# A new order of all work in a fused attention and gated-convolution kernel

## The chip, the cores and the metric

The kernel runs on one core of one Trainium2 chip. The metric is the device time of one execution in microseconds. The kernel before was run three times; the median is the number that a change is held against. One further execution was profiled, and every time of a single instruction in this document comes from that one.

The core has a matrix engine (TensorE, PE in the profile, with its weight loads as PEld), a vector engine (VectorE, DVE), an activation engine (ScalarE, ACT), a general engine (GpSimd, POOL) and a sync engine (SyncE, SP) that here only issues transfers. Each works through its own instructions strictly in the order in which the program gives them. On-chip data lie in SBUF; matmuls write to PSUM, which has eight banks.

## The reference

Two stages, in float32 for the caller, with fp16 operands inside the kernel. First a block-causal attention of 8 batches, 8 heads, 576 positions and head width 64, then a gated projection with a causal convolution of five taps as the gate:

```
scores = q @ k.T / 8
mask   = (pos // 64)[:, None] >= (pos // 64)[None, :]
attn   = softmax(where(mask, scores, -1e9))
x      = (attn @ v)             # heads side by side: 8 x 576 x 512
pre    = sum_k conv_w[k] * shift(x, 4 - k)   # along the sequence, zeros ahead
out    = (sigmoid(pre) * (x @ w_val)) @ w_out
```

## The kernel before

Everything is written as small operations, and a text named PLAN (lines 11 to 74) gives their order. A loop at the end (lines 450 to 454) reads it word by word: `s.4.1@06` calls the operation `s` with the arguments 4 and 1 and the place `06`. A letter after `@` names the engine (A ScalarE, D VectorE, P GpSimd, S the queue of SyncE); digits name PSUM banks. Since each engine keeps the order that it is given, PLAN fixes the order on each of the five queues; between engines only semaphores hold an instruction back, and they are put in for data and for the reuse of buffers and banks.

The operations, with the letters that PLAN uses:

- **Loads** (lines 159 to 187), all DMAs. `Lq.Q` and `Lk.Q` bring four heads of q or k (576 KB) into a ring of six buffers, `qks`; Q runs from 0 to 15, two per batch. `Lv.b.j` brings 128 rows of v of a batch (256 KB), eight buffers; `Lvt.b` its last 64 rows. `Lwv` and `Lwo` bring the two weight matrices in pieces of 512 KB and 256 KB, `Lcw` the taps (10 KB). A load waits until its ring buffer's former content has been cast, and all that stands behind it on the queue waits with it.
- **Casts and turns** (lines 190 to 214): `cq`, `ck` cast a loaded block to fp16, on any of three engines; `dq`, `dk` transpose it on VectorE; `cv`, `cvt` cast v. `wv.x` scales a quarter of the value weights (line 216), `wo.f` casts half of the output weights (line 224). `cwc`, `cw`, `cT` and `DG` turn the taps into small diagonal matrices (lines 386 to 400).
- **Scores** (line 236): `s.Q.t` computes a third of the scores of four heads into two pairs of banks; `sl.b` (line 247) those of the last 64 rows. **Exps** (line 244): `e.p.t` takes one of these pairs of banks, 128x1024, through the exponential on ScalarE; p is a pair of heads, 0 to 31, and p // 2 is Q. `el` does it for `sl`. `m.p` (line 261) clears the masked corners on GpSimd.
- **Attention times v** (line 270): `av.p` is 30 small matmuls into two banks; `n.p` (line 286) divides by the row sums on VectorE. `xtr.p.2` (line 294) transposes two pairs of heads on TensorE, `xt` copies them to SBUF, `xe` copies the last columns of a batch aside.
- **Gate and projection**: `cn.n` (line 321) is the convolution as 80 matmuls on 32x32 tiles, `th` (line 331) the gate as a tanh on ScalarE, `val.n.x` (line 336) a quarter of x @ w_val, `gv` (line 345) gate times value on VectorE, `o.n.t` (line 352) a quarter of the output projection, `oc` (line 360) its copy out of PSUM, `st.n.t` (line 369) the store of two such copies. n is the batch; 8 and 9 gather the last 64 rows of batches 0 to 3 and 4 to 7.
- **Warm-up**: `w.512@b` (line 402) is one 512-column matmul of zeros into bank b whose result nobody reads. `wz`, `id`, `fo` and the words that begin with p set constants and pads.

An operation that writes to a bank waits for whoever reads the bank's former content. So `av.1@4` has to wait for the exp that reads bank 4, and `s.2.0@02` for the two that read banks 0 and 2.

Of the kernel before, what the change touches and what calls it, by code (L numbers as in the profile page):

```python
# [22 lines left out]
val.0.3@2 e.7.2@A gv.0.1@D sl.1@46 dk.4@D gv.0.3@D Lq.5@S cv.1.1@P e.6.2@A cv.1.3@D Lwo.3@S
val.0.2@3 Lvt.2@S gv.0.2@D el.1.0@A cq.4@D px.1@P pp.5@P s.3.0@04 cvt.1@P el.1.1@A e.6.0@A e.7.0@A
Lwo.1@S dq.4@D cv.1.0@P av.5@6 s.3.1@20 n.5@D m.4@P av.4@4 Lv.2.0@S cq.5@D e.7.1@A Lk.5@S e.6.1@A
m.7@P n.4@D m.6@P s.4.0@06 av.7@2 av.6@4 e.8.0@A ck.5@P n.7@D n.6@D e.9.0@A Lk.6@S s.4.1@06 e.8.1@A
Lwo.2@S Lv.2.2@S wo.1@P xtr.4.2@2 Lv.2.3@S Lq.6@S xt.4.2@D wo.0@P e.9.1@A xtr.6.2@4 s.4.2@02 e.8.2@A
xt.6.2@D e.9.2@A m.9@P dq.5@D Lv.2.1@S cn.1@46 val.1.0@0 th.1.0@A dk.5@D xe.1@P gv.1.0@D Lq.7@S
ck.6@P val.1.1@1 s.5.0@24 cq.6@P th.1.1@A e.11.0@A e.10.0@A gv.1.1@D o.0.1@0 oc.0.1@D o.0.2@1
oc.0.2@D cv.2.3@D sl.2@46 el.2.0@A el.2.1@A val.1.2@0 Lvt.3@S cv.2.2@P Lq.8@S s.5.1@24 Lk.7@S  # L30
cvt.2@P Lv.3.2@S e.11.1@A val.1.3@1 m.8@P gv.1.2@D o.0.3@0 dq.6@D dk.6@D s.5.2@46 e.10.1@A cv.2.1@P
Lv.3.3@S e.11.2@A e.10.2@A cv.2.0@P av.8@2 gv.1.3@D n.8@D o.0.0@1 av.9@6 m.11@P s.6.0@24 oc.0.3@D
oc.0.0@A n.9@D av.11@0 st.0.0@S m.10@P cq.8@A e.13.0@A av.10@6 e.12.0@A cq.7@P n.11@D o.1.1@4
cvt.3@P oc.1.1@A n.10@D s.6.1@02 e.13.1@A Lv.3.1@S xtr.8.2@6 xtr.10.2@4 xt.8.2@D Lv.3.0@S xt.10.2@D
# [450 lines left out]
```

## Time and profile before

| | us |
|---|---|
| median of 3 runs | 176.39 |
| lowest and highest | 176.2, 177.06 |
| the profiled execution, device time | 176.23 |
| its span, first to last instruction | 174.4 |
| TensorE busy, share of the span | 161.7, 93% |
| ScalarE busy | 131.5, 75% |
| VectorE busy | 129.9, 74% |
| GpSimd busy | 69.2, 40% |
| moved by DMA | 40.30 MB, mean 231 GB/s |

The device time is 1.8 us longer than the span, for what lies around the first and the last instruction. Matmuls are pipelined and their ends are modelled, so the 93% don't say that TensorE runs at its peak; they say that there are few moments in which it has no matmul under way. "PEclk" and the granted clock are the share of TensorE's full clock that the chip granted.

### The profile page before, as it was taken

How to read it: one execution, taken by the hardware profiler on the slowest of the kernel's cores; microseconds unless marked ns; L12 is line 12 of the kernel's file. 1: busy time of each engine (PE TensorE's matmuls, PEld its weight loads, DVE VectorE, ACT ScalarE, POOL GpSimd, SP SyncE). 2: the span in 40 equal slices, each digit the busy share in tenths (PEclk: the TensorE clock that was granted, in tenths of full speed). 3: DMA queues.
4: the chain of work that ended last, by engine and by line, in shares of the span. 5: the costliest groups of instructions: out<-in, count | busy, mean ns of one | idle time of the engine just before them, and what ended most of it. 6: DMA issues, size and time to landing. Idle time of an engine off the chain costs nothing.

```text
span 174.4 us, 6916 instructions
## 1 busy us (share of the span) xinstructions
PE 161.7 (93%) x3013; PEld 94.8 (54%) x3013; DVE 129.9 (74%) x202; ACT 131.5 (75%) x160; POOL 69.2 (40%) x141
## 2 busy tenths in 40 slices
...
GB/s 176 397 323 296 381 327 195 312 264 301 194 336 271 187 325 334 277 296 319 343 337 242 114 402 198 305 233 357 136 79 2 4 4 194 172 4 120 81 163 241
DMA packets 48216, 40.30 MB, mean 231 GB/s; under 512 B 38453, under 2 KB 38453, under 8 KB 48186
## 3 DMA queue, kind: packets, MB, share of 16 engines
...
HBM read 30.42 MB, written 9.44 MB: 228 GB/s over the span
## 4 chain that ended last, share of the span: by engine, by line
PE 70%; DVE 12%; ACT 7%; issue 5%; DMA 3%; ACTq 0%; DVEq 0%
PE PS L99 65%; ACT pt L242 6%; PE PS L298 5%; DMA qks<-in_q_dram 3%; DVE x L290 3%; DVE qk L156 2%; DVE kT L202 2%; DVE gv L347 2%; DVE qT L202 1%; DVE osb L156 1%; DVE rc L289 1%; ACT osb L156 1%; DVE xt L156 0%; DVE v16t L156 0%; ACT v L156 0%
## 5 line engine op out<-in xcount | busy, mean ns | idle before, releaser
L242 ACT ACTIVATE pt<-PS 128x1024 f16<-128x1024 f32 (+1 forms) x112 | 97.8, 937 | 23.3 <-PE PS L99 20.9
L99 PE MATMUL PS<-qT,kT 32*128 32x64 f16 (+4 forms) x768 | 37.6, 291 | 5.7 <-DVE kT L202 4.5
L99 PEld LDWEIGHTS <-pt 128*128 128x128 f16 x960 | 32.0, 99 | 7.1 <-issue 3.1
L99 PE MATMUL PS<-w_out,gv 128*128 128x512 f16 x144 | 35.3, 380 | 0.1
L347 DVE SCALAR_TENSOR_TENSOR gv<-th,PS 128x512 f16<-128x512 f32 x36 | 24.0, 681 | 14.6 <-ACT th L332 9.3
L156 POOL CAST qk<-qks 128x1152 f16<-128x1152 f32 x22 | 25.3, 1165 | 21.4 <-DVE kT L202 12.3
L99 PE MATMUL PS<-v,pt 128*128 128x65 f16 x896 | 33.0, 195 | 0.9 <-ACT pt L242 0.7
L99 PE MATMUL PS<-xt,w_val 128*128 128x512 f16 x128 | 31.9, 381 | 0.0
L99 PEld LDWEIGHTS <-kT 32*128 32x128 f16 x768 | 16.2, 95 | 28.2 <-issue 16.7
L263 POOL MEMSET pt<- 64x384 f16 x32 | 13.8, 430 | 37.8 <-ACT pt L242 37.1
L290 DVE TENSOR_TENSOR x<-PS,rc 128x640 f16<-128x640 f32 x32 | 26.4, 824 | 1.1
L99 PEld LDWEIGHTS <-w_val 128*128 128x128 f16 x160 | 13.7, 98 | 14.6 <-issue 3.8
L99 PEld LDWEIGHTS <-gv 128*128 128x128 f16 x144 | 12.8, 98 | 14.4 <-issue 0.9
L202 DVE STREAM_TRANSPOSE qT<-qk 128x576 f32<-128x576 f32 x16 | 19.9, 1243 | 0.1
L202 DVE STREAM_TRANSPOSE kT<-qk 128x576 f32<-128x576 f32 x16 | 19.7, 1243 | 0.0
L332 ACT ACTIVATE th<-PS 128x1024 f32<-128x1024 f32 (+1 forms) x20 | 17.7, 947 | 2.2 <-PE PS L99 2.2
L156 DVE COPY osb<-PS 128x512 f32<-128x512 f32 (+1 forms) x20 | 13.4, 671 | 7.3 <-PE PS L99 5.8
L156 ACT COPY osb<-PS 128x512 f32<-128x512 f32 (+1 forms) x17 | 9.7, 583 | 9.0 <-PE PS L99 8.3
L289 DVE RECIPROCAL rc<-PS 128x10 f32<-128x10 f32 x32 | 6.8, 212 | 8.4 <-PE PS L99 5.7
L156 DVE COPY xt<-PS 128x1152 f16<-128x1152 f16 x14 | 10.2, 754 | 3.8 <-PE PS L298 3.7
L156 POOL COPY xtl<-xt 128x272 f16<-128x272 f16 x7 | 3.9, 551 | 22.0 <-DVE xt L156 16.7
L156 POOL CAST v<-vst 128x512 f16<-128x512 f32 x18 | 11.4, 642 | 3.0 <-DMA vst<-in_v_dram 2.4
...
## 6 DMA issues: line engine op xcount, KB each, us to landing
qks<-in_q_dram SPq DMA_DIRECT2D x16, 576.0 KB, 7.0
qks<-in_k_dram SPq DMA_DIRECT2D x15, 576.0 KB, 7.0
...
```

Of the source, the lines that this page charges most:

```text
L99: nc.tensor.matmul(out=out, lhsT=lhsT, rhs=rhs, start=start, stop=stop, skip_group_check=True)
L156: (eng.copy if eng is nc.scalar else eng.tensor_copy)(out=o, in_=i)
L202: m.transpose(out=o.bitcast(fp32)[..., 0], in_=qk16[(2 * Q + i) % NQ16][0:128].bitcast(fp32))
L242: nc.scalar.activation(out=o, in_=i, func=AF.Exp, bias=0.0, scale=0.125)
L263: m.memset(pt[64:128, 0:2, 0:1536].rearrange("p h (t s) -> p h t s", t=3)[:, :, :, 0:64], 0.0)
L289: nc.vector.reciprocal(out=rc, in_=O[:, :, :, 64:65])
L290: nc.vector.tensor_tensor(out=x16[p % NX16][0:128].rearrange("p i h d -> p h i d"), in0=O[:, :, :, 0:64], in1=rc.to_broadcast([128, 2, 5, ...
L298: nc.tensor.transpose(out=f16(bk(m, e))[:, 128 * i:128 * i + 128], in_=x16[(p + e) % NX16][0:128, i, 0:2, 0:64], identity=ident16[0:128, 0 ...
L332: nc.scalar.activation(out=ths[turn(n) % NTH][0:128, 2 * s:2 * s + 2, 0:width(n)], in_=two(slot["cn", n][s])[:, :, 0:width(n)], func=AF.Ta ...
L347: nc.vector.scalar_tensor_tensor(out=gvs[turn(n) % NGV][0:128, e * x:e * x + e, 0:w], in0=ths[turn(n) % NTH][0:128, e * x:e * x + e, 0:w], ...
```

## The change

Only the text of PLAN is replaced. The set of operations that compute something is the same; their order, the engine of some of them and most bank numbers are new. There are 29 warm-up matmuls in place of 17. All first loads are on the queue of SyncE, k ahead of q, where `Lk.0` stood on the queue of ScalarE. `DG` goes from VectorE to GpSimd, `wv.2` from GpSimd to ScalarE and `wv.0` from ScalarE to GpSimd, `wv.3` from VectorE to GpSimd, `cq.3` from GpSimd to ScalarE, `ck.4` from GpSimd to VectorE. In all, 9 casts `ck` are on GpSimd where there were 13, 11 `cq` where there were 9, 23 `cv` where there were 18; all 16 `xt` are on VectorE where 14 were, and 4 `xe` where one was. At the end, the last copy `oc.7.2` is done by ScalarE alone, where the last copy was split over ScalarE and VectorE. The diff, cut to its start (the new order up to about a quarter of the work), the new order around `Lk.9`, and the end:

```diff
-wz@D pk@D pp.2@P Lq.0@S Lk.0@A Lk.1@S Lq.1@S cq.0@D dq.0@D id Lcw@S ck.0@D dk.0@D ck.1@P dk.1@D
-w.512@0 w.512@0 w.512@0 w.512@0 w.512@0 w.512@0 w.512@0 w.512@0 w.512@0 w.512@0 w.512@0 w.512@0
-w.512@0 w.512@0 w.512@0 s.0.2@02 s.0.1@46 tb cq.1@P fo@D Lv.0.0@S e.0.2@A dq.1@D e.1.2@A p4.0@P
-cwc@P s.0.0@02 pv.1@P Lq.2@S e.1.1@A px.0@P cw@6 cT@D Lv.0.3@S cq.2@D e.0.1@A pp.0@P Lv.0.1@S pv.0@P
-e.1.0@A w.512@7 w.512@7 sl.0@64 Lvt.0@S el.0.1@A pp.1@P s.1.2@24 cvt.0@D cv.0.3@D el.0.0@A e.0.0@A
-e.3.2@A Lv.0.2@S cv.0.2@D s.1.0@60 Lk.2@S cv.0.1@P e.3.0@A dq.2@D e.2.0@A Lwv.1@S Lq.3@S p4.1@P
-m.1@P cv.0.0@P av.1@4 m.0@P pp.3@P e.2.2@A s.1.1@06 n.1@D e.2.1@A e.3.1@A Lwv.0@S ck.2@P pp.4@P
-av.0@4 dk.2@D s.2.0@02 n.0@D m.2@P av.2@6 m.3@P Lv.1.0@S cq.3@P e.4.0@A DG@D e.5.0@A av.3@4 s.2.2@02
-wv.1@A n.2@D wv.0@A xtr.0.2@6 n.3@D e.5.2@A xtr.2.2@4 Lk.3@S e.4.2@A Lk.4@S xt.0.2@D ck.3@P s.2.1@26
-e.4.1@A xt.2.2@D xe.0@P wv.2@P ck.4@P wv.3@D Lv.1.3@S e.5.1@A cn.0@04 m.5@P dk.3@D dq.3@D Lv.1.2@S
...
-oc.6.0@A val.7.0@1 gv.7.2@D o.9.0@0 o.9.1@4 gv.7.0@D st.6.1@S gv.7.3@D oc.9.1@A st.6.0@S o.7.0@1
-oc.9.0@D o.7.1@0 o.7.2@2 oc.7.0@A o.7.3@1 oc.7.1@D st.9.0@S st.7.0@S oc.7.2@D oc.7.3@AD st.7.1@SA
+wz@D Lk.0@S Lq.0@S pk@D id Lcw@S p4.0@P cwc@P tb Lq.1@S ck.0@D dk.0@D Lk.1@S Lk.2@S pv.0@P cq.1@P
+Lq.2@S w.512@0 w.512@0 w.512@0 w.512@0 w.512@0 w.512@0 w.512@0 w.512@0 w.512@0 w.512@0 w.512@0
+w.512@0 w.512@0 w.512@0 cw@0 Lv.0.2@S pp.3@P Lv.0.1@S cq.0@D dq.0@D s.0.0@24 cT@D s.0.1@06 dq.1@D
+e.0.0@A ck.1@P dk.1@D fo@D e.1.0@A Lv.0.0@S w.512@2 w.512@2 w.512@2 s.0.2@24 e.0.1@A e.1.1@A Lvt.0@S
+Lv.0.3@S e.1.2@A cq.2@D px.0@P dq.2@D w.512@0 w.512@0 w.512@0 sl.0@06 el.0.0@A el.0.1@A s.1.2@40
+pv.1@P e.0.2@A m.0@P e.2.2@A m.1@P ck.2@D Lwv.1@S cv.0.1@D Lwv.0@S e.3.2@A w.512@6 w.512@6 w.512@6
+s.1.1@62 dk.2@D pp.1@P w.512@4 w.512@4 w.512@4 s.1.0@40 cv.0.0@P pp.2@P pp.0@P e.2.1@A cv.0.2@P
+e.3.1@A p4.1@P pp.4@P e.2.0@A cvt.0@D cv.0.3@P w.512@6 w.512@6 w.512@6 s.2.0@62 m.2@P e.5.0@A av.0@4
+e.3.0@A n.0@D Lq.3@S m.3@P av.1@2 n.1@D Lk.3@S av.2@0 av.3@4 e.4.0@A DG@P n.2@D wv.1@A s.2.2@26
+xtr.0.2@0 wv.2@A n.3@D cq.3@A xtr.2.2@4 e.5.2@A Lq.4@S xt.0.2@D Lv.1.0@S Lvt.1@S wv.3@P xt.2.2@D
+wv.0@P e.4.2@A Lv.1.2@S xe.0@D Lv.1.3@S ck.3@P dq.3@D s.2.1@60 cn.0@24 cq.4@P dk.3@D e.5.1@A e.4.1@A
+Lv.1.1@S cv.1.0@P th.0.0@A val.0.0@0 cv.1.2@P m.4@P cvt.1@D th.0.1@A pp.5@P val.0.3@1 m.5@P Lk.4@S
+Lq.5@S s.3.2@26 cv.1.3@P gv.0.0@D cv.1.1@P val.0.1@0 gv.0.3@D dq.4@D Lwo.1@S e.7.2@A sl.1@46 e.6.2@A
+gv.0.1@D el.1.1@A val.0.2@1 gv.0.2@D Lwo.2@S s.3.1@26 el.1.0@A e.7.1@A av.5@4 e.6.1@A s.3.0@06
+e.7.0@A Lwo.3@S ck.4@D av.4@2 dk.4@D n.5@D px.1@P e.6.0@A s.4.0@64 m.7@P m.6@P Lk.5@S n.4@D av.7@0
+cq.5@P av.6@2 Lwo.0@S e.9.0@A n.7@D n.6@D e.8.0@A s.4.1@46 e.8.1@A xtr.4.2@0 xt.4.2@D ck.5@P Lq.6@S
...
+e.10.0@A cvt.2@P sl.2@26 el.2.1@A el.2.0@A o.0.1@4 oc.0.1@A ck.6@D s.5.1@06 val.1.3@2 e.10.1@A
+Lk.7@S e.11.1@A dk.6@D Lvt.3@S cv.2.1@A gv.1.1@D o.0.0@3 Lk.9@S s.5.2@04 cq.6@P gv.1.3@D o.0.3@2
+oc.0.0@D cv.2.3@D av.8@6 e.11.2@A dq.6@D oc.0.3@A av.9@2 n.8@D e.10.2@A Lq.8@S s.6.0@04 n.9@D m.11@P
+ck.8@A m.10@P av.11@6 ck.7@P e.13.0@A Lv.3.2@S av.10@2 o.1.1@4 n.11@D n.10@D e.12.0@A s.6.1@06
+cq.7@P oc.1.1@A xtr.10.2@2 xt.10.2@D xtr.8.2@4 e.12.1@A xt.8.2@D xe.2@P Lv.3.1@S e.13.1@A s.6.2@02
+cn.2@46 Lv.3.3@S e.12.2@A dq.7@D e.13.2@A o.1.0@0 dk.7@D oc.1.0@D th.2.0@A cvt.3@P m.12@P th.2.1@A
+val.2.2@1 sl.3@24 Lv.4.0@S val.2.3@0 el.3.0@A cq.8@P s.7.0@26 gv.2.2@D gv.2.3@D o.1.2@1 cv.3.2@A
+dq.8@D ck.9@P Lv.3.0@S Lk.10@S cv.3.0@P e.14.0@A el.3.1@A cv.3.3@P e.15.0@A o.1.3@0 s.7.2@24
...
+n.28@D av.30@0 xtr.28.2@2 n.30@D xt.28.2@D av.31@6 n.31@D o.6.2@5 o.5.3@0 xtr.30.2@2 st.5.0@S
+oc.6.2@A xt.30.2@D oc.5.3@D o.6.3@1 xe.7@P oc.6.1@D o.6.0@5 val.9.1@0 oc.6.0@A cn.9@26 st.6.0@S
+th.9.1@A th.9.0@A gv.9.1@D val.7.0@4 val.9.0@5 cn.7@26 oc.6.3@A st.6.1@S th.7.0@A val.7.3@0
+val.7.2@1 gv.9.0@D st.5.1@S th.7.1@A val.7.1@5 gv.7.0@D gv.7.3@D gv.7.2@D gv.7.1@D o.9.1@4 o.9.0@0
+o.7.0@1 o.7.1@5 oc.7.0@D oc.9.0@A o.7.3@0 oc.7.1@D oc.9.1@A st.9.0@S oc.7.3@A st.7.0@S o.7.2@1
+oc.7.2@A st.7.1@AS
```

More of the change, by code (lines that the diff above doesn't have):

```diff
@@ L23 @@
[L23 to L34, printed above, removed]
@@ new lines @@
+av.20@2 Lk.15@S oc.3.3@D av.21@0 n.20@D Lq.14@S n.21@D o.4.0@6 oc.4.0@A m.23@P Lv.7.3@S s.12.0@24
+Lv.7.0@S cq.14@D e.24.0@A m.22@P e.25.0@A xtr.20.2@0 xt.20.2@D av.23@6 av.22@2 s.12.1@04 n.23@D
+n.22@D o.4.1@6 e.24.1@A Lq.15@S oc.4.1@D xtr.22.2@2 o.3.2@7 e.25.1@A s.12.2@04 xt.22.2@D oc.3.2@A
+e.24.2@A cn.5@26 ck.14@P st.3.0@S o.4.2@0 cv.6.2@P e.25.2@A th.5.1@A dk.14@D dk.13@D st.4.0@S
+dq.13@D val.5.0@1 oc.4.2@D th.5.0@A gv.5.0@D s.13.2@46 Lv.7.2@S val.5.1@0 gv.5.1@D val.5.2@1
+e.26.2@A sl.6@24 ck.15@D e.27.2@A cv.7.2@P m.24@P el.6.0@A o.4.3@0 gv.5.2@D cv.6.1@P s.13.0@26
@@ new lines @@
+el.6.1@A oc.4.3@A m.25@P o.8.1@1 e.26.0@A e.27.0@A val.5.3@0 oc.8.1@A s.13.1@24 e.27.1@A Lv.7.1@S
+dq.14@D cq.15@P gv.5.3@D cv.6.0@D cvt.6@P st.3.1@S o.8.0@6 dq.15@D e.26.1@A m.27@P o.5.0@7 oc.5.0@A
+s.14.0@04 e.28.0@A cvt.7@P oc.8.0@D av.24@2 dk.15@D n.24@D m.26@P av.26@6 av.25@0 n.26@D e.29.0@A
+s.14.1@24 o.5.1@6 e.29.1@A n.25@D oc.5.1@D e.28.1@A av.27@0 s.14.2@46 xtr.24.2@2 n.27@D e.28.2@A
+xtr.26.2@0 xt.24.2@D s.15.1@42 e.29.2@A xt.26.2@D e.31.1@A cn.6@06 st.4.1@S e.30.1@A o.5.2@2
+oc.5.2@D val.6.0@3 th.6.1@A th.6.0@A xe.5@D sl.7@46 xe.6@P el.7.1@A gv.6.0@D val.6.2@2 cv.7.1@D
```

60 lines of the change are left out of this document (22 added, 38 removed).

## The prediction

> **What bounds the kernel now.** I read the page first, its busy times and the shares of the chain that ended last:
>
> ```profile
> PE 161.7 (93%) x3013; PEld 94.8 (54%) x3013; DVE 129.9 (74%) x202; ACT 131.5 (75%) x160; POOL 69.2 (40%) x141
> ...
> PE 70%; DVE 12%; ACT 7%; issue 5%; DMA 3%; ACTq 0%; DVEq 0%
> ```
>
> TensorE carries the span. An average hides the stages, so I cut the span at events of the plan: first scores, first `av`, `s.2.2`, `s.4.1`, last matmul. The columns are the stretch, its length, each engine's busy time with its count, the granted clock, the DMA share and GB/s:
>
> ```profile
> 0.00:10.75 10.75, 5.01 (x15) 1.78 (x16) 5.00 (x10) 1.49 (x2) 3.67 (x11) 1.00 0.86 304
> 10.75:18.68 7.93, 7.00 (x87) 2.60 (x88) 6.71 (x12) 7.11 (x9) 5.17 (x19) 0.54 1.05 305
> 18.68:25.63 6.95, 6.67 (x144) 5.53 (x144) 4.69 (x8) 6.76 (x8) 3.64 (x8) 0.79 1.09 362
> 25.63:41.41 15.78, 15.07 (x335) 9.80 (x333) 15.04 (x23) 14.66 (x18) 10.39 (x19) 1.00 0.99 268
> 41.41:170.15 128.74, 127.95 (x2439) 75.11 (x2436) 97.99 (x151) 101.09 (x123) 46.37 (x88) 1.00 0.68 208
> 170.15:174.43 4.28, 0.00 (x0) 0.00 (x0) 0.42 (x1) 0.37 (x1) 0.00 (x0) 1.00 0.65 242
> ```
>
> Three regimes. Up to 10.75 us TensorE has only warm-ups and then waits for data. From 10.75 to about 41 us ScalarE sets the pace: 28.5 us busy of 30.7 (7.11 + 6.76 + 14.66), while TensorE runs at 0.54 and 0.79 of its clock in the first two of these stretches. From 41.41 us on TensorE is busy for 127.95 of 128.74 us; nothing but less matmul work or fewer pauses helps there, and of visible pauses there is 0.8 us. The last 4.28 us are the last copy and store. So a new order can move time in the first 41 us and in the tail; in the 129 us between it can mostly lose.
>
> **First scores.** The timeline of the start, DMA issues among it (start, duration, engine, line, operation; in brackets the idle time before and what ended it):
>
> ```profile
> 0.74 0.41 ACTq L161 DMA_DIRECT2D qks<-in_k_dram  x1
> 0.74 0.39 SPq L161 DMA_DIRECT2D qks<-in_q_dram  x1
> ...
> 1.23 5.01 PE L99 MATMUL PS<-wz 128*128 128x512 f16 x15 [1.23 <-DVE wz L408]
> ...
> 6.23 0.76 DVE L156 CAST qk<-qks 128x1152 f16<-128x1152 f32 x1 [4.84 <-DMA qks<-in_q_dram]
> 7.03 1.26 DVE L202 STREAM_TRANSPOSE qT<-qk 128x576 f32<-128x576 f32 x1
> 7.65 1.14 POOL L156 CAST qk<-qks 128x1152 f16<-128x1152 f32 x1 [6.19 <-DMA qks<-in_k_dram]
> 8.13 1.28 DVE L156 CAST qk<-qks 128x1152 f16<-128x1152 f32 x1
> 9.07 1.33 POOL L156 CAST qk<-qks 128x1152 f16<-128x1152 f32 x1 [0.28 <-DMA qks<-in_q_dram]
> 9.44 2.33 DVE L202 STREAM_TRANSPOSE kT<-qk 128x576 f32<-128x576 f32 x2
> ...
> 10.44 0.60 POOL L156 CAST conv<-conv_nat 5x512 f16<-5x512 f32 x1
> ...
> 10.75 1.42 PE L99 MATMUL PS<-qT,kT 32*128 32x320 f16 x32 [4.51 <-DVE kT L202]
> ```
>
> q0, k1 and q1 are taken up at 6.23, 7.65 and 9.07, each by an engine that waited for it: 1.42 us per 576 KB load. Four loads in 9.07 means that data flow from about 9.07 - 4 x 1.42 = 3.39, and q0 and k0, issued at once on two queues, share the first 2.84 us. One after the other, as the change has them, k0 comes at 4.81 and q0 still at 6.23; the second issue on SyncE costs 0.4 us of its queue and is hidden in the 3.39. VectorE then does the four steps in a row: cast 4.85 to 5.61, turn to 6.91, cast to 7.70, turn to 9.0. Scores start at 9.05 where they started at 10.75: **-1.7 us**. A cast beside GpSimd's took 1.28 in place of 0.76, so up to 0.5 of it can go to GpSimd's pads. If one load alone is no faster than two together, k0 comes at 6.2, and the scores start at 10.4; that is the other end.
>
> The change adds one wait ahead of them: `cw` now stands before `s.0.0` on TensorE, and all of TensorE's work is behind it. It needs the 10 KB of taps, third on the queue, whose landing no row shows; between q0 and q1, so 6.2 to 7.65, plus the cast of 0.60 gives 8.25 at the latest, 0.8 us ahead of the scores. I count nothing. Later loads are the same bytes on a queue that is full anyway (share 0.86 to 1.09 in the first four rows); v comes behind q2 now, up to 1.4 us later, but its first reader `av.0` is after 20 us.
>
> **ScalarE from the first exp to `s.4.1`.** Its timeline:
>
> ```profile
> 11.42 7.11 ACT L242 ACTIVATE pt<-PS 128x1024 f16<-128x1024 f32 x9 [8.74 <-PE PS L99]
> 18.70 2.85 ACT L242 ACTIVATE pt<-PS 128x1024 f16<-128x1024 f32 x3 [0.17 <-PE PS L99]
> 21.73 3.77 ACT L242 ACTIVATE pt<-PS 128x1024 f16<-128x1024 f32 x4 [0.17 <-PE PS L99]
> 25.38 1.15 ACT L220 ACTIVATE w_val<-th 128x512 f16<-128x512 f32 x2
> 26.42 3.96 ACT L242 ACTIVATE pt<-PS 128x1024 f16<-128x1024 f32 x4
> ...
> 32.44 2.49 ACT L242 ACTIVATE pt<-PS 128x1024 f16<-128x1024 f32 x4 [0.23 <-POOL pt L264]
> ...
> 35.44 5.67 ACT L242 ACTIVATE pt<-PS 128x1024 f16<-128x1024 f32 x6 [0.50 <-PE PS L99]
> ```
>
> Both plans have the same 16 activations ahead of the weight scaling, 7.11 + 2.85 + 3.77 = 13.73 us. The first exp came 0.67 us after the scores began, so now at 9.72; without the two pauses of 0.17 the sixteenth ends at 23.45. The scores are ready in time, as each `s` gets its banks one exp or more ahead of its own exps. Then come the two scalings (1.15, to 24.6) and, new on ScalarE, `cq.3`:
>
> ```profile
> L156 ACT CAST qk<-qks 128x1152 f16<-128x1152 f32 x3 | 3.5, 1154 | 0.0
> ...
> L222 POOL TENSOR_SCALAR w_val<-th 128x512 f16<-128x512 f32 x1 | 1.5, 1494 | 0.0
> ...
> L399 DVE TENSOR_TENSOR DG<-idfold,convT 128x640 f16<-128x640 f16 x1 | 0.8, 817 | 0.0
> ```
>
> 1.15 more, to 25.8, so `e.5.2` starts near 25.9 where it started at 26.42: -0.5. TensorE keeps up if its clock is full (the first row is an `av` at the reduced clock, the second the same at full clock):
>
> ```profile
> 18.68 1.48 PE L99 MATMUL PS<-v,pt 128*128 128x65 f16 x24
> ...
> 24.62 0.90 PE L99 MATMUL PS<-v,pt 128*128 128x65 f16 x24
> ...
> 25.63 0.64 PE L99 MATMUL PS<-qT,kT 32*128 32x320 f16 x16
> ...
> 27.66 0.75 PE L99 MATMUL PS<-qT,kT 32*128 32x448 f16 x16
> ...
> 41.41 0.64 PE L99 MATMUL PS<-qT,kT 32*128 32x448 f16 x16
> ...
> 164.81 5.34 PE L99 MATMUL PS<-w_out,gv 128*128 128x512 f16 x24
> ```
>
> The four `av` wait for the banks of `e.2.0`, `e.5.0` and `e.3.0`, which end at 20.6, 21.6 and 22.5; at 1.0 us each (24.62 to 25.63) they end at 24.6, and `s.2.2` starts 1.0 earlier than at 25.63. So ScalarE, not TensorE, ends last here. From there I shift its rows: four exps, two tanh, then the pause of 0.23 at 32.44 all but goes, since the scores wait for nothing later than ScalarE itself; the pause of 0.50 stays. That gives `s.4.1` at 40.7 in place of 41.41: **-0.7 us**. Of the lead of 1.7, one us is eaten by `cq.3` on ScalarE.
>
> `DG` on GpSimd has no row. Below, VectorE's 0.82; above, GpSimd's slowest elementwise row, 1.49 for 512 columns, which makes 1.87 for 640. I take the upper. It starts after `m.3` at about 23.2; two weight scalings of 1.49 follow, to 28.05, and `val.0.0` asks for them at 29.3, `cn.0` for `DG` at 27.9: free either way. The Trainium skill, "GPSIMD Engine Reference", section "Performance versus the Vector engine", gives 2.6 cycles per element for a two-input operation; an estimate from it is 640 x 2.6 / 1.2 GHz = 1.39 us, which would leave the sum as it is.
>
> **From `s.4.1` to the last matmul** the same matmuls stand in nearly the same pattern (scores, `av`, `xtr`, `cn`, then values and projections between them). Moved casts and copies lighten VectorE a little and load GpSimd, which is busy for 46.37 of 128.74 us, so has room. I count 0. Visible pauses bound a gain by 0.8; at the share lost from 25.63 to 41.41, 0.71 of 15.78, a loss would be 5.8 - 0.8 = 5 us. I stay near 0, as this very stage is the nearest row, and keep 1 us to either side.
>
> **Tail.** The six last projections stand back to back as before (24 matmuls in 5.34). Behind them, before and for the kind of copy that takes its place:
>
> ```profile
> 167.60 0.59 ACT L156 COPY osb<-PS 128x512 f32<-128x512 f32 x1 [0.28 <-PE PS L99]
> ...
> 170.23 0.37 ACT L156 COPY osb<-PS 128x256 f32<-128x256 f32 x1 [2.05 <-PE PS L99]
> 170.64 0.42 DVE L156 COPY osb<-PS 128x256 f32<-128x256 f32 x1 [0.62 <-ACT osb L156]
> 171.09 0.36 ACTq L376 DMA_DIRECT2D out_dram<-osb  x1
> ```
>
> The two halves of the last copy didn't run together: VectorE's began when ScalarE's was done. Last matmul at 170.15, last store issued at 171.09: 0.94. One whole copy on ScalarE takes 0.08 + 0.59 + 0.03 = 0.70: **-0.2 us**. If the order ahead of it leaves a hole (`xt.30`, `xe.7` and `gv.7` have about 0.25 us of cover each), it is +0.3.
>
> **The sum**, on the profiled execution's 176.23: -0.7 in the first 41 us, 0 in the middle, -0.2 in the tail: 175.33, say **175.3 us**. The median, 176.39, is 0.16 above the profiled time, so this is -0.6% of it.
>
> **Rivals.**
>
> *The clock falls again, and the added warm-ups become the bound.* This is the one that ends slower. Shares of 0.54 and 0.79 mean, between full and half rate, about 7.3 of 7.93 and 2.9 of 6.95 us at half rate, after TensorE had stood from 6.24 to 10.75. Now it stands from about 6.0 to 9.05, with four tiny matmuls between, and up to 20 us it is busy about half of the time, three warm-ups between scores included: for it, the gap is still 3 us; against it, it was 4.5 before. If half rate holds from 11 us until after 20 us, three 512-column matmuls cost 1.3 us (twice 5.34/24 each) and a score step about 1.0. From `s.1.2` at 14.9 on TensorE then has three score steps and three threes of warm-ups in a row (3 x 1.0 + 3 x 1.3), so `s.2.0` starts at 21.8; the four `av` at full rate again end at 26.5, the sixteenth activation at 25.4, and with 2.3 for scalings and cast `e.5.2` starts at 27.7, 1.8 after my forecast: **177.1 us**. It decides at 18 us: if the rate is back by then, nearly nothing is lost. The Trainium skill, "TensorE: Matmul & The Clock Gate", section "Part 1: The HAM clock gate (the "warmup" mystery)", says that a free-running window of some 3.4 us sets full or half rate, one idle window for the fall and one busy one for the rise. The shares here agree as mixtures of full and half; by that rule a gap of 3 us can't fill a window, which speaks for the forecast, but where a window begins is left to each execution, and no row shows how little work counts as idle. Chance 0.20.
>
> *The change doesn't do what it says: k0 comes no earlier*, since one load alone doesn't fill the DMA engines at the start. Against it, k1 and q1 came 1.42 us apart, each alone at the head of its queue; for it, nothing flows before 3.39, and whether a single load gets through that start-up faster than two no row shows. Scores at 10.4, 1.35 later than forecast: **176.7 us**. Chance 0.12.
>
> *The lead is kept whole.* `cq.3` falls into a moment in which ScalarE would have waited anyway (its pauses of 0.23 and 0.50 say that there are such), and the lead of 1.7 reaches TensorE's stage: 176.23 - 1.7 - 0.2 = **174.3 us**. For it, TensorE has `s.2.2` ready 1.0 us earlier already; against it, 28.5 of 30.7 us busy on ScalarE leave little. Chance 0.15.
>
> *A pause in the long stage.* A load that waits for a buffer holds all behind it: `Lk.9` now stands on the queue where `ck.6` has only just freed its buffer, with `Lq.8` and five v loads behind.
>
> ```profile
> qks<-in_k_dram SPq DMA_DIRECT2D x15, 576.0 KB, 7.0
> ```
>
> 7.0 us from issue to landing at 1.42 us per load means that nearly five loads are under way, so a short wait is covered; if the wait outlasts them, `av.12` waits for its v by what is left, a load's 1.42 us and more, above 177. Chance 0.08.
>
> **Chances.** Forecast 0.45, with its own range of 174.7 to 175.9 (0.6 to either side, the 0.5 of the slowed cast and the pause of 0.50). A measurement of this kernel can tell about 0.5%, 0.88 us, so faster means below 175.5, slower above 177.3. Two thirds of the forecast's case and the whole lead are faster: 0.31 + 0.15 = 0.46. No change: 0.14 of the forecast, 0.12 of the clock, 0.09 of the load: 0.35. Slower: the rest, 0.19. The range that leaves out the pause and a few hundredths of the outermost clock and lead cases is 174.0 to 177.3; the 1 us of the middle is within it for the forecast.
>
> **What would show it.** Right: first scores near 9.05, first exp near 9.7, granted clock above 0.9 from 10 to 25 us, `e.5.2` near 25.9, `s.4.1` near 40.7, the last store issued 0.7 after the last matmul. Wrong in the first step: VectorE's first cast after 6 us. Wrong in the second: a granted clock near 0.5 between 11 and 20 us, with TensorE busy without a break from 15 us on, and ScalarE waiting for it. Wrong in the third: stretches after 41 us with TensorE's pauses well above 0.8 us in all. Wrong altogether, though every step holds, if the tight middle gives the lead back in pieces of a tenth.

## The result, and the profile after

| | before | after |
|---|---|---|
| median, us (4 runs each, side by side) | 176.72 | 179.49 |
| lowest and highest | 176.2, 177.28 | 178.98, 179.86 |
| span of the profiled execution | 174.4 | 178.1 |
| `s.0.0` starts | 10.75 | 8.82 |
| `s.4.1` starts | 41.41 | 39.97 |
| last matmul ends | 170.15 | 173.82 |

The changed kernel takes 1.0154 times as long, 95% interval 1.011 to 1.0199. Medians here and below are of all runs; a ratio goes by the fast ones alone, those within 1.5% of their kernel's fastest. The changed kernel is slower by 2.8 us where 1.1 us of gain was forecast, though it is ahead by 1.44 us at `s.4.1`. The page of the changed kernel:

```profile
span 178.1 us, 6919 instructions
PE 163.0 (92%) x3025; PEld 95.5 (54%) x3025; DVE 129.3 (73%) x196; ACT 131.2 (74%) x162; POOL 70.6 (40%) x144
...
PEclk9999999999999999999999699999999999999998
...
q8 instruction: 23, 0.38, 0.8%
```

The clock is full from 6 us on, but one slice of it, at about 100 us, stands at 0.6. The line on q8 was in the page of before too (23 packets), and I passed over it: 0.38 MB in 23 packets is 16.4 KB each. TensorE's 6050 instructions, matmuls and weight loads, make 23.6 pieces of 256, so a packet fits 256 instructions of 64 bytes. My reading is that TensorE's own program comes in by DMA; the experiments below bear it out.

The start, in the timeline of the changed kernel, does better than forecast:

```profile
8.82 1.08 PE L101 MATMUL PS<-qT,kT 32*128 32x512 f16 x24 [1.71 <-DVE convT L158]
...
9.49 13.49 ACT L244 ACTIVATE pt<-PS 128x1024 f16<-128x1024 f32 x16 [7.25 <-PE PS L101]
22.76 1.24 ACT L222 ACTIVATE w_val<-th 128x512 f16<-128x512 f32 x2
23.80 1.23 ACT L158 CAST qk<-qks 128x1152 f16<-128x1152 f32 x1
24.84 2.03 ACT L244 ACTIVATE pt<-PS 128x1024 f16<-128x1024 f32 x2
```

The sixteen exps run without a pause, and `e.5.2` comes at 24.84. The loss is behind. The two kernels cut at the same places (stretch, length, busy times with counts, granted clock, DMA share, GB/s), first the changed one:

```profile
39.97:44.00 4.03, 2.80 (x55) 1.89 (x52) 2.62 (x5) 1.94 (x2) 2.96 (x3) 1.00 1.13 330
44.00:88.00 44.00, 43.67 (x831) 24.87 (x828) 36.62 (x52) 40.21 (x51) 21.48 (x40) 1.00 0.96 272
88.00:98.00 10.00, 7.20 (x191) 4.90 (x191) 6.15 (x8) 6.49 (x8) 3.91 (x8) 1.00 1.02 294
98.00:110.00 12.00, 11.95 (x245) 7.78 (x242) 9.99 (x17) 7.92 (x9) 3.48 (x7) 0.86 0.78 220
110.00:173.82 63.82, 63.78 (x1128) 37.01 (x1126) 44.67 (x70) 43.26 (x54) 15.79 (x35) 1.00 0.41 130
173.82:178.10 4.28, 0.00 (x0) 0.00 (x0) 0.00 (x0) 0.59 (x1) 0.00 (x0) 0.87 0.64 241
```

and before:

```profile
41.41:44.00 2.59, 2.43 (x51) 1.77 (x52) 2.17 (x5) 1.85 (x2) 1.14 (x1) 1.00 1.11 220
44.00:88.00 44.00, 43.57 (x838) 24.63 (x831) 35.51 (x53) 37.30 (x45) 25.29 (x45) 1.00 0.97 290
88.00:98.00 10.00, 10.00 (x264) 7.22 (x261) 8.41 (x15) 8.29 (x11) 3.41 (x6) 1.00 0.78 234
98.00:110.00 12.00, 11.93 (x203) 5.96 (x200) 10.18 (x15) 10.73 (x14) 3.48 (x7) 1.00 0.86 280
110.00:170.15 60.15, 60.01 (x1097) 35.54 (x1096) 41.72 (x68) 42.92 (x54) 13.05 (x29) 1.00 0.39 130
```

From `s.4.1` to the last matmul the changed kernel takes 133.85 us, before 128.74: 5.11 more. TensorE's idle time there is 1.23 + 0.33 + 2.80 + 0.05 + 0.04 = 4.45 against 0.80, so 3.65 more. It comes from two short stretches: 1.07 more from 40 to 44 us and 2.80 more from 88 to 98 us, and 0.22 less elsewhere. The rest is the clock: 0.86 over 12 us is one window of 3.41 us at half rate, 1.7 us of work lost. Together that is 5.35, or 0.24 more than the 5.11; what gives the 0.24 back I don't know. TensorE's own timeline shows both stops and the slow rows behind the second:

```profile
42.01 1.18 PE L300 MATMUL PS<-ident,x 128*128 128x128 f16 x18 [1.19 <-issue]
...
93.55 0.94 PE L101 MATMUL PS<-xtl,w_val 128*128 128x256 f16 x7
97.04 0.28 PE L101 MATMUL PS<-xtl,w_val 128*128 128x256 f16 x1 [2.55 <-issue]
...
98.88 1.50 PE L101 MATMUL PS<-v,pt 128*128 128x65 f16 x24
100.19 0.24 PE L101 MATMUL PS<-v16t,pt 128*128 128x65 f16 x1
```

The stops stand in the middle of an operation. `xtr.4.2` stops after 2 of its 10 transposes (the row of 18 goes on into `xtr.6.2`), `val.8.0` after 7 of its 8 matmuls: same inputs, same bank, no datum to wait for, and the releaser is "issue". What was missing, then, is the next instruction. The DMA view of the changed kernel, first from 88.3 to 94.6 us, has one queue only:

```profile
DMA packets 1648, 1.95 MB, mean 309 GB/s; under 512 B 1150, under 2 KB 1150, under 8 KB 1648
...
q1 hardware_dynamic: 1648, 1.95, 102.2%
```

and from 94.6 to 95.6 us:

```profile
q1 hardware_dynamic: 577, 0.32, 105.4%
q8 instruction: 1, 0.02, 6.0%
```

The packet of the piece starts at 94.62, and 2.4 us later TensorE goes on. Over all 23 pieces of the trace a pattern fits: piece k is asked for when TensorE is at about its instruction 256k + 185, since behind the last load, from 130 to 165 us, the packets start between 0.3 us before and 1.1 us after that one; TensorE runs dry at about 256k + 445; and a piece can be used 2.2 us or more after its packet starts. The place of asking is fitted, so a wait worked out from it is an estimate, good to about 1 us. By this reading (call it theory I) the piece of the second stop was asked for at 88.25 and waited 6.4 us for the DMA engines, that of the first was asked for at 34.75 and waited 4.7. In before the same two waited 3.9 and 1.3. The margin from asking to running dry is about 6 us at these two; less the 2.4 and 2.6 us from packet to use, a wait of up to some 3.5 us is free there.

### The profile page after: what moved, and what is told of

Same layout as the page of the kernel before. It is cut to its first block, busy times and chain, and to the rows that moved or that the text cites. A ratio compares the mean times of both kernels' runs of the same rounds, so it can differ in the third digit from the quotient of the medians.

```text
span 178.1 us, 6919 instructions
## 1 busy us (share of the span) xinstructions
PE 163.0 (92%) x3025; PEld 95.5 (54%) x3025; DVE 129.3 (73%) x196; ACT 131.2 (74%) x162; POOL 70.6 (40%) x144
## 4 chain that ended last, share of the span: by engine, by line
PE 75%; DVE 8%; ACT 8%; issue 4%; DMA 2%; DVEq 0%
PE PS L101 70%; ACT pt L244 8%; PE PS L300 5%; DVE xt L158 2%; DMA qks<-in_k_dram 2%; DVE x L292 2%; DVE qT L204 1%; DVE qk L158 1%; DVE kT L204 1%; DVE xtl L158 1%; DVE rc L291 0%; DVE gv L349 0%; ACT osb L158 0%; DVE v16t L158 0%; DVE convT L158 0%
## 5 line engine op out<-in xcount | busy, mean ns | idle before, releaser
L101 PE MATMUL PS<-qT,kT 32*128 32x64 f16 (+4 forms) x768 | 35.2, 279 | 2.5 <-DVE convT L158 1.7
L265 POOL MEMSET pt<- 64x384 f16 x32 | 14.5, 452 | 49.8 <-ACT pt L244 49.1
L101 PEld LDWEIGHTS <-kT 32*128 32x128 f16 x768 | 15.3, 93 | 24.0 <-issue 16.8
L158 POOL CAST qk<-qks 128x1152 f16<-128x1152 f32 x20 | 22.8, 1150 | 5.1 <-issue 3.5
L101 PEld LDWEIGHTS <-w_val 128*128 128x128 f16 x160 | 14.2, 98 | 17.8 <-issue 5.5
L158 ACT COPY osb<-PS 128x512 f32<-128x512 f32 x21 | 12.3, 589 | 14.3 <-PE PS L101 12.7
L158 POOL CAST v<-vst 128x512 f16<-128x512 f32 x23 | 14.5, 647 | 9.7 <-PE PS L101 9.3
L158 DVE COPY xt<-PS 128x1152 f16<-128x1152 f16 x16 | 11.7, 752 | 4.2 <-PE PS L300 3.6
L158 DVE COPY osb<-PS 128x512 f32<-128x512 f32 x15 | 10.2, 687 | 5.1 <-PE PS L101 2.5
L300 PE MATMUL PS<-ident,x 128*128 128x128 f16 x160 | 11.4, 220 | 1.4 <-issue 1.2
```

Source lines behind the costliest of these rows:

```text
L101: nc.tensor.matmul(out=out, lhsT=lhsT, rhs=rhs, start=start, stop=stop, skip_group_check=True)
L158: (eng.copy if eng is nc.scalar else eng.tensor_copy)(out=o, in_=i)
L265: m.memset(pt[64:128, 0:2, 0:1536].rearrange("p h (t s) -> p h t s", t=3)[:, :, :, 0:64], 0.0)
L300: nc.tensor.transpose(out=f16(bk(m, e))[:, 128 * i:128 * i + 128], in_=x16[(p + e) % NX16][0:128, i, 0:2, 0:64], identity=ident16[0:128, 0 ...
```

## The experiments

Two readings stand against each other. Theory I: loads under way hold up TensorE's instructions, and the loss is the stops and the half-clock window. Rival II: the new order is worse by itself, above all in when its loads come, and the stops go along with it.

The table gives, for the profiled execution of each kernel, TensorE's remaining work less that of before at the same time. I price each of TensorE's steps (a score step, an `av`, a `val` and so on) with its usual distance from start to start, and add up those not yet begun; below zero is ahead of before. The two waits are those of the pieces asked for at about 35 and 88 us. One row is one execution, and that can lie well to either side of its kernel's median: those of e10 and e11 took 2.0 and 3.8 us more than theirs, those of e4 and e12 2.6 and 1.8 more, those of e13 and e14 1.5 and 1.4 less. For e2 the waits are left out, since its pieces begin elsewhere.

| kernel | 24 us | 40 us | 48 us | 90 us | 106 us | end | first wait | second wait | median |
|---|---|---|---|---|---|---|---|---|---|
| changed kernel | -1.43 | -1.27 | -0.41 | -0.07 | 3.86 | 3.67 | 4.7 | 6.4 | 179.49 |
| e1_hold | -1.25 | -1.09 | 1.86 | 1.85 | 2.62 | 3.38 | 5.8 | 3.2 | 180.25 |
| e2_phase | -1.56 | 0.24 | 1.13 | 2.10 | 3.54 | 3.34 | | | 179.51 |
| e3_nowarm | -0.16 | 0.01 | 1.57 | 2.19 | 4.06 | 3.88 | 5.7 | 5.0 | 179.82 |
| e4_first | -1.86 | -0.85 | -0.01 | 2.00 | 2.34 | 2.43 | 4.2 | 2.3 | 176.12 |
| e7_tinyonly | -1.29 | -1.14 | -0.10 | -0.09 | 1.18 | 1.62 | 3.9 | 3.7 | 177.35 |
| e10_late | -0.36 | -0.21 | 2.54 | 2.39 | 2.93 | 7.39 | 5.4 | 2.1 | 181.44 |
| e11_both | -1.04 | -0.30 | 2.26 | 2.13 | 2.82 | 8.09 | 5.6 | 2.4 | 180.25 |
| e12_first2 | -2.06 | -0.42 | 0.28 | 1.10 | 1.84 | 1.90 | 5.5 | 2.7 | 176.29 |
| e13_late2 | -1.32 | -1.17 | 1.36 | 1.27 | 2.15 | 2.42 | 5.1 | 3.6 | 180.07 |
| e14_front2 | -1.28 | -1.12 | -0.89 | -1.00 | 0.69 | 0.33 | 0.4 | 2.6 | 177.83 |
| e15_both2 | -0.89 | -0.74 | -0.40 | -0.14 | 0.23 | -0.15 | 0.5 | 4.0 | 176.24 |

The kernel before beside these runs took 176.76 (e1 to e4), 177.09 (e5 to e8), 176.98 (e9 to e12) and 177.24 (e13 to e16).

**One load later, and the pieces shifted.** In e1 one store that has to wait stands ahead of a load at 84 us:

```diff
-e.21.0@A Lq.12@S
+e.21.0@A st.2.1@S Lq.12@S
...
-st.2.1@S e.22.1@A
+e.22.1@A
```

> The new order with one word moved: the store st.2.1 stands ahead of Lq.12, so that the queue of SyncE waits for oc.2.2 (to about 88.8 us) before it issues Lq.12 and what follows. TensorE's own order is untouched. Theory I (TensorE's instructions are fetched by DMA in pieces of 16 KB, wait behind the loads, and came too late at 94.5 us; the stop of 2.55 us then halved the clock for 3.4 us): by 88.8 us only loads up to Lv.5.1 are under way, which landed by 91.5, so the piece lands ahead of 94.3; stop and half clock both go, 2.6 + 1.4 = 4.0 us less: about 175.4 us. Rival II (the clock falls there by itself, the stop has to do with what TensorE executes): the time stays within 0.5 us of 179.5. Rival III (the stop is an unnamed wait for data or for a bank): no change either, as no data of val.8.0 are touched.

Measured 180.25, with four runs from 177.89 to 181.05. The second stop is gone, as its timeline shows, all eight matmuls in one row:

```profile
43.55 1.25 PE L300 MATMUL PS<-ident,x 128*128 128x128 f16 x10 [2.52 <-issue]
...
96.19 1.05 PE L101 MATMUL PS<-xtl,w_val 128*128 128x256 f16 x8
```

but the first stop, ahead of which this kernel is the same as the changed one, took 2.5 us in place of 1.2 and brought the half-clock window. The time that I expected missed since I took the first stop for a constant.

In e2 the 14 warm-ups of 512 columns at the start become 56 of 128, the same array time, so that all later pieces begin 84 instructions earlier in the work:

```diff
-w.512@0   (14 times)
+w.128@0   (56 times)
```

> The new order with the 14 first warm-ups of 512 columns replaced by 56 of 128 columns: the same columns, 84 more instructions of TensorE's two kinds, all before 8 us. Everything else as it is. Theory I: the borders of the fetched pieces move 84 instructions towards the front of the work, so the stop that was ahead of the last matmul of val.8.0 is now found inside s.9.1, near 91 us, and the loads are as thick there, so it is 2 us or longer; total 179 to 181.5 us. Rivals II and III: the stop stays at the last matmul of val.8.0, at the same length, total unchanged within 0.5 us.

179.51. The stop at `val.8.0` went to `s.9.1`, as expected, in the middle of its 16 matmuls, but it is 1.17 us long where I expected 2 or more:

```profile
92.89 0.60 PE L101 MATMUL PS<-qT,kT 32*128 32x448 f16 x9
94.66 0.24 PE L101 MATMUL PS<-qT,kT 32*128 32x64 f16 x7 [1.17 <-issue]
```

(What e2 loses ahead of 42 us are two pauses of 0.9 and 0.5 us at 37 to 39 us, both for VectorE, and a half-clock window behind them.) The place of a stop follows the count of instructions, not the operation. That is the mark of a fetch in pieces. The page of e2 has 24 packets on q8, and each of the other kernels, with 84 to 114 instructions of TensorE fewer, has 23:

```profile
q8 instruction: 24, 0.39, 0.8%
```

The traces of all 18 kernels say the same. Behind 20 us they have 18 pauses of TensorE of 0.5 us or more that are named "issue", in eleven kernels. Each begins when the number of TensorE's matmuls and weight loads so far, counted in order of start, leaves 188 to 190 on division by 256, whatever the operation there, and each ends 2.2 to 3.9 us after the packet of that piece starts. Rivals II and III of e1 have no reason for that.

**The start alone.** e3 takes the 15 warm-ups between the first scores away; e4 gives before only the new sequence of first loads:

```diff
 (e3)
-w.512@2 w.512@2 w.512@2   (and four more such threes)
 (e4, on the kernel before)
-Lq.0@S Lk.0@A Lk.1@S Lq.1@S cq.0@D dq.0@D id Lcw@S ck.0@D dk.0@D
+Lk.0@S Lq.0@S Lk.1@S Lq.1@S ck.0@D dk.0@D id Lcw@S cq.0@D dq.0@D
```

> The new order without the 15 warm-ups that stand between the first scores and exps (the 14 at the start stay). My prediction held that they keep the clock up and cost nothing while it is up. If they are what keeps it up: the granted clock is near 0.5 somewhere between 10 and 24 us, and s.2.2 starts 1 us or more later than at 24.12. If the short gap alone keeps it: s.2.2 starts within 0.3 us of 24.12. By theory I there are also 30 instructions fewer, so the stop of val.8.0 moves 30 instructions on, into av.17, and is some 0.5 us shorter; by rivals II and III it stays where it is.

> The old order with one part of the change: both first loads on the queue of SyncE, k0 ahead of q0, and VectorE casting and turning k0 first. If the lead of the first scores is worth what I predicted, they start near 9.0 and the first exp near 9.7 where it was 11.42, and with cq.3 still on GpSimd up to 1.5 us reach the end: 175.2 to 176.0 us. If half clock sets the pace until 21 us anyway, the lead is lost by s.2.2: 176.4 to 177. By theory I a lead of TensorE shortens the cover of its instruction pieces (by 0.1 us at 43 us before), so up to 1 us of it can be paid there.

e3 took 179.82, ratio 1.0153 (1.0092 to 1.0215). Its clock is half from 10.2 to 23.9 us, and it stands 1.3 us behind the changed kernel at 24 us. At the end it is 0.2 behind. It has 30 instructions fewer, and its late stop lies at the same count, now inside `av.17` as expected, though only 0.35 us long. e4 took 176.12, ratio 0.9956 (0.9922 to 0.9989): some 0.7 us gained out of 1.9 us of lead. In its trace, whose execution took 178.67, TensorE waits at 47 us for the cast of the output weights:

```profile
PE PS L99 <- POOL w_out L156: 2.1, 1, 2.1
```

So I brought `Lwo.2` forward and two v loads with much to spare back (e12):

```diff
-Lvt.2@S ... Lv.2.0@S ... Lk.5@S ... Lk.6@S ... Lwo.2@S
+Lk.5@S Lwo.2@S ... Lk.6@S Lvt.2@S Lv.2.0@S
```

> The kernel before with its first loads in sequence on SP, as in e4_first, and with the last output weight Lwo.2 ahead of Lk.6, and Lvt.2 and Lv.2.0 (13 us to spare) behind Lk.6, since in e4_first's trace o.0.1 waits 2.1 us at 47 us for the cast of the output weights, Lwo.2 landing at 46.9. The lead of the start was 1.9 us at 24 us and 0.85 us at 42 us there. If the start's lead is a gain by itself: 175.2 us, faster than before by 0.7 us or more. If a lead in the start is lost again to whatever is late next: 176.2 within 0.5.

176.29, ratio 0.9972 (0.9938 to 1.0005), the second of the two outcomes. The chain of e12 says where the lead went:

```profile
28.90 9.17 DMA qks<-in_q_dram
```

From 29 to 38 us the chain is one q load that stands in line. The DMA share is 1.0 or so from 5 to 50 us in before and in the changed kernel, so a lead at 24 us probably meets loads that can't come earlier. e3 would be the same from the other side.

**Pacing all loads.** If backlog is the cause, less of it should help everywhere. From `Lq.5` on, a 4-byte DMA ahead of each load reads the buffer of the load three (e5) or two (e6) places back, so that SP waits for its landing. e7 has the same small DMAs reading something that landed long ago; e8 is e5 on the kernel before:

```diff
+        nc.sync.dma_start(out=scr[0:1, n:n + 1], in_=landed(*loads[-3]))
```

> The changed kernel; from the 21st input load on (Lq.5, some 27 us) the loads are paced: ahead of each, a 4-byte DMA on SP reads the buffer of the load three places back, so that SP waits until that load has landed and no more than three are under way. Order of all work as in the changed kernel. Theory I (TensorE's instructions come in pieces of 256 by DMA on queue q8, each piece waits behind the loads that are under way, and a piece that comes too late stops TensorE and then costs a half-clock window): the waits of the pieces fall from 3 to 6.4 us to about 2 us, the stops at 40.8 us (1.2) and 94.5 us (2.5) go and with them the half-clock window (1.45): 179.5 - 5.2 = about 174.3 us. Rival II (the new order of loads is itself what costs, the stops are a by-product): pacing delays loads further, 179.5 or more.

> As e5_pace3, but with the load two places back, so that no more than two are under way. Theory I: waits of the pieces of 1 to 2 us, no stop for instructions; but with two loads under way the transfers no longer fill the DMA engines, and from 27 to 48 us, where loads land 0.4 to 4 us ahead of their use, casts begin to wait: between 174 and 178. Rival II: slower than the changed kernel, above 180.

> Control for e5_pace3: the same 4-byte DMAs at the same places, but each reads a buffer that landed long ago, so that nothing is held back. Theory I: the stops stay, 179.5 us within 1. If the gain of e5_pace3 came from the small DMAs themselves (SP slowed by 0.4 us at each), this one would show it too.

> The kernel before, with the pacing of e5_pace3 in the same way. It has no stop in its profiled run (least slack of a piece 0.1 us, at 43.2 us), so theory I gives little: 175.8 to 176.8 us. Rival II: the later loads cost, above 177.

192.39, 215.77, 177.35 and 187.0. Theory I was wrong on e5, e6 and e8 by 10 us and more, since I took the holds for free. In e5 SP waits for a landing ahead of 30 of the 56 small DMAs, up to 3.4 us and 34.2 us in all, and issues no load meanwhile; v casts come late (TensorE's waits in e5):

```profile
PE PS L101 <- POOL v L158: 5.6, 3, 2.5
PE PS L101 <- ACT pt L244: 2.7, 7, 0.7
PE PS L101 <- DVE xt L158: 2.0, 1, 2.0
```

No wait of e5 is named "issue", but it bought that with late data. The control e7 missed too, on the good side: ratio 1.0005 (0.9953 to 1.0056) where I expected the changed kernel's time. Most of the small DMAs take SP 0.6 us each, and so they space out the loads; the second piece waited 3.7 us, and the late stop shrank to

```profile
93.67 0.94 PE L101 MATMUL PS<-xtl,w_val 128*128 128x256 f16 x7
94.82 0.28 PE L101 MATMUL PS<-xtl,w_val 128*128 128x256 f16 x1 [0.21 <-issue]
```

The early stop is still there with 1.0 us, and no half-clock window follows behind 14 us. Nothing but the small DMAs was changed in e7, and 2 us were gone.

**Holding back what has time.** In e10 the loads with 7 to 34 us to spare between 78 and 105 us wait for exps, by a 4-byte DMA that reads the exp's output; e11 also holds `Lwo.0` until `e.7.1`:

```diff
 (e10; G.p.t@S waits for e.p.t)
-Lv.5.2@S ... Lv.5.1@S ... Lq.12@S ... Lk.13@S ... st.1.1@S Lv.6.3@S ... Lvt.6@S ... Lv.5.0@S ... Lvt.7@S Lq.13@S Lv.6.2@S
+Lq.12@S st.1.1@S G.19.1@S Lv.5.2@S Lv.5.0@S Lv.5.1@S ... G.20.0@S Lq.13@S Lk.13@S Lv.6.3@S ... G.21.2@S Lvt.6@S Lv.6.2@S
 (e11 besides)
+G.7.1@S Lwo.0@S
```

> The changed kernel, with the loads that have 7 to 34 us to spare between 78 and 105 us held back: Lv.5.2, Lv.5.1, Lv.5.0 go behind a 4-byte DMA on SP that waits for exp e.19.1 (some 92 us), Lk.13 and Lv.6.3 behind one that waits for e.20.0, Lvt.6, Lv.6.2 and what follows behind one that waits for e.21.2. Theory I: the pieces asked for at 81.6, 88.3 and 103 us wait 1 to 3 us instead of 4.7, 6.4 and 2.7; the stop at val.8.0 and its half-clock window go, 179.5 - 4 = 175.5 us; the stop at xtr.4.2 (41 us) stays. Rival: the held loads come late and TensorE waits for v or q casts near 97 to 110 us, 178 or more.

> As e10_late, and Lwo.0 and the loads behind it wait for exp e.7.1 (some 35 us) in the same way, so that fewer loads lie ahead of the piece asked for at 34.8 us. Theory I: that piece waits about 3 us instead of 4.7, the stop at xtr.4.2 goes too, 174.3 us. Rival: the front is bound by the loads themselves, Lwo.0 and Lq.6 land later and o.0.1 or s.5 waits: 176 or more.

181.44 and 180.25. Both mechanisms came true at once. The second stop is gone: from 90 to 106 us e10 loses 0.5 us where the changed kernel loses 3.9. But `Lv.6.3` now lands too late for its cast, VectorE waits, and behind it `gv` and the projection (timeline of e10):

```profile
110.26 0.86 DVE L158 CAST v<-vst 128x512 f16<-128x512 f32 x1 [3.12 <-DMA vst<-in_v_dram]
...
111.76 1.27 PE L101 MATMUL PS<-w_out,gv 128*128 128x512 f16 x3 [2.78 <-DVE gv L349]
```

The hold of e11 at the front came too late in the queue: four large loads were already ahead of the piece, and it waited 5.6 us.

**The two holds made right.** e13 has only the first hold of e10, with `Lv.6.3` ahead of it. e14 brings `Lk.5` ahead of the output weights and holds these until `e.7.1`. e15 has both:

```diff
 (e13)
-Lv.5.2@S ... Lv.5.1@S ... Lq.12@S ... Lk.13@S ... st.1.1@S Lv.6.3@S ... Lv.5.0@S
+Lq.12@S st.1.1@S Lv.6.3@S G.19.1@S Lv.5.2@S Lv.5.0@S Lv.5.1@S Lk.13@S
 (e14)
-Lwo.1@S ... Lwo.2@S ... Lwo.3@S ... Lk.5@S
+Lk.5@S G.7.1@S Lwo.1@S Lwo.2@S Lwo.3@S
```

> The changed kernel with the hold of e10_late at one place only: Lv.6.3 and st.1.1 go right behind Lq.12, then SP waits for exp e.19.1 (some 92 us) before Lv.5.2, Lv.5.0, Lv.5.1 and Lk.13; the later loads as in the changed kernel (in e10_late a v load held too long made DVE and then o.3.0 wait 2.8 us). Theory I (pieces of TensorE's instructions wait behind loads): the piece asked for at 88.3 us waits 2 us, val.8.0 goes through at once, TensorE's remaining work stands against before's as it did at 90 us still at 106 us, that is 4 us less than in the changed kernel: about 175.7 us, or 1.3 to 2 more where the stop at xtr.4.2 reaches 2 us and brings a half-clock window. Rival (the late stage of the new order is worse by itself): 178 or more.

> The changed kernel with Lk.5 ahead of the output weights, and Lwo.1, Lwo.2, Lwo.3 and what follows behind a 4-byte DMA on SP that waits for exp e.7.1 (35.3 us). Theory I: at 34.8 us one load is under way rather than seven, the piece asked for then waits 1 to 2 us instead of 4.7 and the stop at xtr.4.2 (1.2 to 2.5 us) goes; but the DMA engines are full from 5 to 50 us, so the 1 to 2 us in which they idle come back as late casts before 55 us: gain of the first 0 to 1.5 us, the late stop stays; 178 to 180 us.

> e13_late2 and e14_front2 together. Theory I: neither stop; 174.5 to 176 us. If the front stays bound by the loads, as e13_late2.

e13: 180.07, ratio 1.0129 (1.0071 to 1.0188), above what I expected; its profiled execution took 178.58. The late stop is gone in it (0.9 us lost from 90 to 106, and a stop of 0.6 at the piece before, at 91 us), the early one is there with 1.6 us and its half-clock window. e14: 177.83, ratio 1.0025 (0.9982 to 1.0067), lower than expected. At 35 us its DMA engines are nearly free and the piece is there at once (from 34.9 to 35.8 us):

```profile
q8 instruction: 1, 0.02, 6.4%
q1 hardware_dynamic: 2, 0.00, 1.3%
```

`xtr.4.2` isn't stopped, and the weights that land some 4 us later, and `Lq.6` 2 us later, cost nothing that can be seen: the table has e14 still 1.0 us ahead of before at 90 us. The stop at `val.8.0` stayed away too, but one of 1.05 us came at 104 us, in the middle of `val.4.3`:

```profile
105.17 0.82 PE L101 MATMUL PS<-xt,w_val 128*128 128x512 f16 x3 [1.05 <-issue]
```

e15: **176.24**, ratio 0.9971 (0.9933 to 1.001), 0.2 us above the range I expected. Its span of 174.1 us has no stop longer than 0.2 us and no late half-clock window (page, then the stretch of the second stop):

```profile
span 174.1 us, 6921 instructions
...
PEclk9978999999999999999999999999999999999999
```

```profile
90.00:110.00 20.00, 19.88 (x369) 11.91 (x365) 16.61 (x27) 17.11 (x21) 9.22 (x16) 1.00 0.92 249
```

Two holds in SP's queue and a few loads moved there, with every computing instruction in its place, take the changed kernel's loss away. That speaks against the first half of rival II: its order of computing is as good as before's as long as no piece is late. The second half, when its loads come, is what e15 changes too; there theory I says why that costs, and it is the place of the stops that decides for it.

**The reverse.** Can loads ahead of a piece make a stop in before? e9 issues four v loads twice behind `Lv.6.1`, e16 two loads of 512 KB:

```diff
 (e9)
+Lv.6.1@S Lv.5.3@S Lv.5.2@S Lv.5.1@S Lv.6.3@S
 (e16; X.i brings 4 KB rows of q into the idle buffer of the output weights)
+Lv.6.1@S X.0@S X.1@S
```

> The kernel before, with four v loads issued a second time (Lv.5.3, Lv.5.2, Lv.5.1, Lv.6.3, the same data into the same buffers, used some 10 us later or more) behind Lv.6.1 at some 87 us, so that about 3.7 us of loads more lie ahead of the instruction piece that TensorE asks for at 90.0 us; nothing else. Theory I (pieces of TensorE's instructions wait behind loads): that piece waits about 4 us instead of 1.3, TensorE stops for about 1.5 to 2 us at some 94.3 us with no wait named, a half-clock window may follow, 178 to 180 us. Rival (what costs in the changed kernel is its order of work): before's order with 1.3 MB more of loads loses nothing or waits on a load that comes late, 176.7 within 0.7, and no stop for instructions.

> The kernel before with two loads of 512 KB in rows of 4 KB (into the buffer of the output weights, which is not read any more) behind Lv.6.1 at some 87 us; e9_extra with large rows, since over the runs so far a q or k load under way goes with 0.9 us of waiting of a piece and a v load with 0.5. Theory I: the piece asked for at 90.0 us waits about 3.5 us instead of 1.3, TensorE stops 1 to 2 us at 94.3 us with no wait named: 177.5 to 179.5 us. If loads that lie ahead do not hold up the pieces: 176.7 within 0.7, no stop there.

177.02 and 176.6, ratios 1.0 (0.9964 to 1.0035) and 0.9989 (0.9954 to 1.0024): no stop at that piece, waits of 2.1 and 1.2 us. Theory I missed both. SP's issue rows show why the test was weak: in e16 its issues took up to 3.0 us each around 90 us, so the added loads only pushed the next ones later, and `X.0` was issued over 89.6 to 92.6 us, when the piece had been asked for at 92.1. About four transfers were under way then, with or without more behind them. A stop made at will in before is not shown. Stops do come in before's order, at the piece of 43 to 45 us: 0.16 us in before itself, 0.49 in e16, 0.63 in e9 and 0.95 in e12, none of which was meant to have one there.

## Why the prediction was wrong

- **First scores at 9.05** (-1.7): right. 8.82, -1.93; k0 landed at 4.47 and q0 at 6.06, each before the forecast's 4.81 and 6.23. The row of the first scores names `convT`, done at 8.79, but `s.0.0` reads the turned q0, done at 8.77, and no bank of the taps; `cw` itself ran at 6.87, so the taps cost nothing, as counted.
- **First exp 9.72, `e.5.2` 25.9**: right in kind, off in size. 9.49 and 24.84. The forecast added durations; in the row, sixteen exps take 13.49 us where the sum of before's rows was 13.73, and the two scalings and `cq.3` overlap the next by some 0.2 each. `cq.3` ate less of the lead than the one us I gave it. `DG` on GpSimd took 1.26 us where I had taken 1.87, and it was free either way.
- **`s.2.2` 1.0 earlier, `s.4.1` 40.7** (-0.7): too cautious. 24.12 and 39.97, so -1.5 and -1.44: up to there it went as in the rival *The lead is kept whole*, all but 0.5 us.
- **The clock rival** didn't come: full clock from 6 us on, and in the variants with all warm-ups one or no half-clock window at about 10 us. e3 shows that the added warm-ups did that (without them four such windows in a row), and that in the changed kernel, with its stops, it was worth next to nothing at the end.
- **"From `s.4.1` to the last matmul ... I count 0", with 1 us to either side**: this is the step that failed. It took 5.11 us more, and the sign named for it came: 4.45 us of pauses. The same fraction worked out from the stage ahead had given a possible loss of 5 us, and I set it aside because the long stage of before showed pauses of 0.8 us. That row was evidence on before's margins only. At 94 us its piece had some 0.8 us to spare, and at 43 us it was late already, in the middle of `xtr.6.2`, which follows `xtr.4.2` (timeline of before):

```profile
43.16 0.55 PE L298 MATMUL PS<-ident,x 128*128 128x128 f16 x7 [0.16 <-issue]
```

I counted that 0.16 among the pauses without asking what it was, and passed over the q8 line. The runs put in its place: waits of up to 6.4 us for TensorE's instructions, two stops (1.2 and 2.5 us) and 1.7 us of half clock. e15, which changes only when loads are issued, has neither such a stop nor that half-clock window, and comes back to before's time.
- **"A pause in the long stage"** had 0.08 and the wrong cause, a v load held up behind `Lk.9`. `av.12` didn't wait.
- **Tail, -0.2**: the step was right, 0.65 us from the last matmul to the last store's issue, where before took 0.94, but it isn't in the span: 4.28 us behind the last matmul in both. That store landed 2.52 us after its issue, before 2.25. Why was not tried.
- **Whether a lead at 40 us reaches the end** I took for granted. e15 has no stop and still loses 0.3 us of its lead from 40 to 48 us and the rest by 106; e3, e4 and e12 suggest that the loads of 5 to 50 us decide there. Even without the stops the change may have been worth some tenths of a us; e15 against before can't be told from no change.

What stays open is what sets the length of a single wait. Over ten of these traces, 230 pieces, a rough fit of mine gives 0.75 us and 0.9 more for each q or k load under way, 0.7 for a store or a weight, 0.5 for a v load, with an error of 0.95 us. The 6.4 us of the second stop lie far outside it: when it was asked for, a load of q, a store and two v loads were under way, the last of them to 92.9 us, and others were issued while the piece waited to 94.6.
